# A gated linear recurrence and an MLP: the first batch's small gate operations on another engine, and a new order of all work

## The chip, the cores and the metric

The kernel runs on one core of one Trainium2 chip. A core has five engines that run their own instruction streams in order and meet through semaphores: TensorE (PE, matrix products), VectorE (DVE), ScalarE (ACT), GpSimd (POOL), and SyncE (SP), which here starts all DMA transfers. The metric is the device time in microseconds (us), the median over runs of the same program. A separate execution was profiled: its time is given beside the runs, and all durations come from it.

## What is computed

Two blocks follow each other. The first is a linear recurrence with complex decay, for 4 batches, 8 heads, 768 tokens and 48 channels. Cut to what matters:

```python
mag = np.sqrt(a_re * a_re + a_im * a_im)
scale = np.minimum(mag, 0.999) / (mag + 1e-06)
for t in range(S):                       # S_re, S_im: one 48 x 48 state per head
    new_re = ar * S_re - ai * S_im       # ar, ai: the scaled a_re, a_im of token t
    new_im = ar * S_im + ai * S_re
    S_re, S_im = new_re + kv, new_im     # kv: outer product of k and v of token t
    y[t] = q[t] @ S_re
```

The second takes the result as 3,072 tokens of 384 values and runs an MLP over it: `h = x @ w_in` (to 2,048 features), `g = max(h, 0) + alpha * min(h, 0)`, `g @ w_out` (back to 384).

## The kernel before

**Gates.** The decays are turned into running products. This is done in nine groups of tokens, `gates(g, b, c0, c1)`: chunks of 128 tokens 0, 1 to 2 and 3 to 5 of batch 0 are groups 0, 1 and 2; each later batch has two groups of three chunks. A group loads its slices of `a_re` and `a_im` (L248), normalizes them with ScalarE and VectorE (L251 to L308), and forms products over blocks: wide ones within blocks of 8 tokens, smaller ones over blocks of blocks, and a serial run over the ends of these (`product`, L336 and L338; the serial run is the loop over `nr`, which is 2, 4 and 6 steps long in groups 0, 1 and 2). Between these stages ScalarE makes negated copies (`three`, L364 and L366; L389). Then follow corrections of the offsets (L394, L397), a renormalization (L401 to L407), and the wide products L422 and L425. The decays go to `decs` in DRAM (L321), the rotations to `phs` (L417, L427). A `carry` links a group to the next of its batch.

**Who does the small operations.** `tiny` and `tiny_engine` (L230) choose an engine for a group's small operations: the products whose width is at most `SMALL` (80), the serial run, the offsets' corrections and the renormalization. In the kernel before it is VectorE for group 0 alone and GpSimd for the other eight.

**Units.** A unit is one chunk of 128 tokens, all heads; there are 24. `loads` brings q and k (`KQ`, three buffers), the rotations (`PP`, one buffer, L586) and the decays (`T`, two buffers, L593); `loads_v` brings v in the layouts that are needed. `unit(u)` then rotates KQ (L645), and goes through six levels of halves: TensorE multiplies (`ps_lv`, L659), VectorE multiplies KQ by decays (L698), ScalarE copies a half (`W`, L716), the products are masked (L680, L683). Then come transposes (`ps_kt`, L733), the new states (`ps_kv`, L746, with L754 and L757 on VectorE), and y, from the carried state (L773) and from the levels (L786). y goes to DRAM (`ysc`) and comes back transposed as `xT`.

**Weights.** `w_in` and `w_out` come as 64-bit numbers in 16 pieces (L487) and are turned into 32 bits by ScalarE (L503 to L507) and VectorE (L511 to L515).

**MLP.** The units' tokens are taken in 14 groups: two of one unit, ten of two, two of one. For each group and each of 16 blocks of 128 features, `features` runs three products (`ps_h`, L833), ScalarE a relu (L840) and VectorE the rest of the activation (L842); `outputs` adds up the 16 products with `w_out` (`ps_o`, L852), one block behind the features. `ps_h` has two buffers.

**The order.** Each of these tasks is a generator that yields between instructions. The string `ORDER` has one letter for each step (A to I: gate groups; J: loads; K: the copies of v into half rows; L: loads of v; M: weight loads; N and O: the two weight conversions; P to Z and a to m: units 0 to 23; n: loads of x; o: the MLP), and `plan.run(ORDER)` advances the named task. So the string fixes how every engine's queue is filled, and the DMA queue too. It was found beforehand by a search over a model with durations; the search isn't part of the kernel.

Of the kernel before, what the change touches and what calls it, by code (L numbers as in the profile page):

```python
# [27 lines left out]


ORDER = (  # L30
    "AAAAAAAAAAAAAAAMMAMJMMBJBAAAAAAAAAAAAAAAAAAAOOONNAAAAAAAAAAMAAAAAABNAAAAAAAAAAANAAAAABOAAAAAAAAJNABA"
    "ANAMBAAMAJAAAAAAAAAKNBBBBNNBBBBMBBBBBBBBBBBBCCBOOOBBBBBBBBBBBBBBBBBBBBBBBBBBBKJJJKONNOONOOPNCCCNNNBB"
    "OBOKPNNMNNNOOCONBBBBLLLBBBBBJPPPPPOCCKLKKLNNLPPCCCPCPPPKMKOCCPPCPOKKKKKBBBBBBBPBCBBBOBBJKPPOCMNPOONN"
    "NNBCMOJOLLLLCLPOMMMNPPPPPLLBBBBBBBCBCBBBBBBBNPCNCPJJLJDDJJPCCCJPKPCCCCCCCCCCCPPCCCPPPNCCCNCCCCCCCCPP"
    "NNPPJPPPOPNODJOPPPOJQDNPOPPCCCCCCPDQQQOQDDNNOODQQQOQDQQMJDCQCCCCCCQOODQJJDCQQQKDCDDDDCCCDCOnRCKKCKCD"
    "QooooJKKQQJJOooMJoQooooooCCCQCCLNDoRCCDooCRRRoOoooooooDQCRRDNoRooooooooooooDRQoKOQKQCRCoQLLLLQoDRooL"
    "oLoLLLLLLLQoQCCDDoRRDDJKQooMKCCCCCCNCDDQQQNoooQQCCoNQooooCoQQQQQQQQQQQQCDCooLNoOnoooJRRoORNoooOoooLo"
    "oooOooRooooJJJONDLRLDoEooooooOoooDoooooDooRooJooooooSRDoooooRRRRRooooRooRRooDLLLLLLLLLLoooEooJoDDSoo"
    "SoRSDSSoDDDRoSSoRoRoDooDSoDoRRRRRRJRoSEoSRERESERSRRRJJJoSSJToSESooooESSooSoRTEoSRDJDDDSSDKDSDDJDDDDD"
    "DDDDDDTESTTLDDRSSSToLLLooTLEoEDDDoETSooooLoLLJJLLLLLLoTSooEoSTRoooSoSEEESoSSSESSTKKDDDDDDKKDDDoDDDSS"  # L40
    "SSSESJJKoJoSJUJSSKooSoooDooooooTLLJnTETJLEEEKKEETJTDDEooDDDDooooooooLEUDEDooooToUUUDooEDTEoooLoooooo"
    "oUooTDTDLEooooTTTDTEDoooooTooooTUoooEoJooTLLoETETUoEDTTUUoUTooEooUoooEoEULLLLLLTTTTTTTEEJTooTTTTTTTJ"
    "FEEEFJEEEEUUoEoooooEEVooEoUUUUUUVVFoooooooUVUoUUFoTUUJTJEVVoFooFoEEEUUooooLUVUUVoVVFooVLLELLLLLLLLLL"
    "UUFEVoUEEEFUUUUUEUJVVJJJJVVUUoooUFUVJEEEVWoVoVVVVVEVVEooEooWJJEEEEEWoVoVoUoKWWVVVWVVVFWWFWFEEEoEEEoE"
    "EEFULLLLLLLLLLLLoLLVWVFVWWVVVVVVVWnVWFFJooooooEoWJJJJJWoLLLLLKoXLoooooWWoJWWWWEEEEWFooKooLLLLLLLoXEW"
    "WWooooVEEVoWEFVLWWEoooooEVJJJKWJVEoEEooWoWoWWVEWXoooooXooooooWWWWWWWFFFEXWWWWXoXJoXFLLLLLLFWWGGJJoWo"
    "FFFFoFFoFooFFooooXFoooXoXooFFoooXXXoXLXooLoFJooooKFFXooooGFFXooXGoGoXXXXooooGFoFYoGXoGooooFooooooYGG"
    "XXXGooooooGFFoooooooXGGoXLXGLJonYYYGooGooXXGFoFLoLFLFLoYXYXXYXoooXXXYoJJJJJYJJooooXFFFFFFFYYYXFXXGoo"
    "FFFFGGYGJoGooGGYGLLZLLLLLLLYLLoooLoLFLoooFYoooXFFYYFoooooGoJGGGGFFXGZYGYXYXFFYXXYYYYYooFFFFFoooGYYGG"
    "GGGZoooooYoFFFFFoFoooFoooYYZoYooZZGYYYYYYYJJJJJJoZZGGYYGoZFLGGLZLLLLZZFooooKLLLGJFFGJYaZooKFoFFKooGG"  # L50
    "GoFooYZoooGGZKFoooooFFoooooZZZoKZoYYZYYZZZZooooooLooLooaGGGGGZZooLFoZFFooLFoZGGZGGGGGGGGGnooooooZZoo"
    "ooooZaLaaZZFZaooaJaZoooZGaoaZZZZZZJJJGaGGGaaaaoJJJGGGGGGGJJGGabbaoooooLLLLLoooooooooooooooooooZGbZZo"
    "LLLLLLLLGbKaGHGaobobHZGGGZaaGGGoaboooooooooooooooaGaabaJaaooZoooGoGaboooaaaooooaabbbaabaaaGJbJaaJJbJ"
    "LbJHbaoLoocaaHboLooboJJooHoaaoHHoJKLbaoooHoobbbbbboooGoooooooooLocbbcoooHbbooooooHHHKHHLLHbLbLcooooo"
    "ooooLnooooLbobLLLcooHooobbbGIcccbJbcbIbbbbJbbbJJbbbbccJoooooooooooHHoHHccoIoooooccoooIodooHccooooooo"
    "HcLcdoooJooooHHHHHHHodcoJooooooccccddooccoccdddoocooccocLdLLooooLLLLLLLLJLLcdccdJJddcccHcccccccccccd"
    "eJdHooooHoooooooodJdHHHHooooooooddoeoddddeedoooooooooedHeoHddeIooooooddodoHIHHKooKoddeeooLLLLLLLLLLL"
    "LLLdddIneeeddedHddddddddeeeeooHHoJJoKJJJJfoJoIdKdJooooooooooIoHHoooodfIefoooeHHHHHHHHeooHooeofeeefJI"
    "oIoooooJooooooIIofeeHHHIHHIKoooeHeIfKJHHJoeoooHHHoooooooooooeHHHHHooHHHofeooLLLLLLLLLLLLLLJJofeeeeff"
    "ffeeeHHHHeeeeeeeeffgJJJfeKKKKoeLfoooHHJoHHoooooooHHooIgffHfLLLLLLLffLggLLffooKJLHooeoLoooooIgogfIgoI"  # L60
    "IIHoIfoHIIfILnHHHHoooooooooooooooKoofggoJfoofoooHoHooofooffHHHHHffoooooooooofooooooggIggIIIIIfffffff"
    "fIJgoILIoooooggoooogooJILILIILILLoogoIooLoggffgggooooffofoIIoIIhoooooogoooooooLoohIhhggggLLoooggJJLo"
    "oLLJJoogoooooooooJJJJIooogohhhggghggggJgIgIIIhhhhgggIIIggooIoohIIhLIIIIoioohgIIIoooooIIIIIIIIoohhhoo"
    "ooooJhhhhiiihhhLLLLhioLLooooooooIIILJihhLLJLIILIILIoioJoJLohhIhoJohhJiiohnoooiIihihhoooohjooooohhiIh"
    "IIhIIhhhJJhijiooLLIoioooIoIooooojIooooooooooooIojoooJooLoLLLLLLLLLiiijjjojhjooooooLooooooooIIIoooooi"
    "IIjiiiiJJijiioooooooooiiohLoooooohojohooJooihjiioooooiJJooiiiiiiiiiiiiiijJJLLioiJoLjJkojooLooooLoLLL"
    "oJjJonooLLooojLLJjkkjjkkjjoJLjoooooLoooooooojjjkkookooooojjoojoooojoojjjlkkjkkkjjjjjjjjjjjjjokkkJooo"
    "okoooooooooooolLLJkkooooooookkkkllkoooooooooolklkoolooLLllJoooooLLoooLLJoooooooLLkjkooooooooLoookkoo"
    "oookkooLooooooooLLkkokllJllkkJJkkkkkkkkJlkkkkooooooollooooooooomlooooooomJlllnJlolmmlLLLlooLmLLLLLLL"
    "LLoooooooLooloommoooloooolomlloooooloooloooooooolllmmlmmmllllllllmmoooooooooooooolmmllmmoomoommooooo"  # L70
    "oollloooooooooooooomomLooooooooooooooooooooooooooooooooooooommonoooooooooooommmoooooooooooooooooooom"
    "moLLooooooooooooooooooooLLLooLLooooooomoooLLLLoLmoomoooooooommmmmmmmmmmmmooooooooooooonooooooooooooo"
    "oooooooooooooooooooooooooooooooooooooooooooooooooooooooooooooooooooooooooooooooooooooooooooooooooooo"
    "oooooooooooooooo")

# [27 lines left out]
def kernel(  # L103
# [32 lines left out]
    nc = tc.nc  # L136
# [62 lines left out]
    DVE = ACT = POOL = PE = DMA = step  # L199
# [21 lines left out]
    def gates(g, b, c0, c1):  # L221
# [3 lines left out]
        first, last = c0 == 0, c1 == NCH  # L225
# [1 line left out]
        STT = nc.vector.scalar_tensor_tensor  # L227


        tiny, tiny_engine = (DVE, nc.vector) if b == 0 and first else (POOL, nc.gpsimd)  # L230

        def small(k, *after):
            return tiny(k, *after) if k <= SMALL else DVE(k, *after)
# [660 lines left out]
    with tc.manual_schedule():  # L894
        for i, g in enumerate(GATES):
            plan.add(gates(i, *g))
        plan.add(loads())
        plan.add(half_rows())
        plan.add(loads_v())
        plan.add(pieces())  # L900
        plan.add(weights("in"))
        plan.add(weights("out"))
        for u in range(NU):
            plan.add(unit(u))
        plan.add(loads_x())
        plan.add(all_mlp())
        plan.run(ORDER)
# [37 lines left out]
```

## Time and profile before

| | |
|---|---|
| median of 3 runs | 895.61 us (893.58 to 896.97) |
| the profiled execution | 889.42 us |
| its span, first to last instruction | 887.7 us |
| granted TensorE clock, mean | 0.962 |
| TensorE busy | 712.9 us (80%) |
| VectorE busy | 645.7 us (73%) |
| ScalarE busy | 428.0 us (48%) |
| GpSimd busy | 227.4 us (26%) |
| bytes moved by DMA | 130.98 MB, mean 148 GB/s |

The profile is a page of parts. The first gives each engine's busy time, its share of the span and its instructions. The second cuts the span into 40 equal slices; a digit is the busy share of a slice in tenths, and PEclk is the clock that TensorE was granted, in tenths of full speed. The third lists the DMA queues; queue 8 carries instructions. Behind the page lies the trace: what each engine waited for (with the time, the number of waits and the longest), sums over chosen stretches, and lists of instructions in order of time, with start, duration, engine, source line, operation, tiles and shapes. "issue" stands for time in which an engine waited for nothing that the profile shows. A matmul of 32-bit numbers appears as two records on PE and two weight loads on PEld.

### The profile page before, as it was taken

The numbers are of one execution on the slowest core, as the hardware profiler recorded it, in microseconds if no ns is written. First come the engines' busy times: TensorE is split into PE (matmuls) and PEld (weight loads), VectorE is DVE, ScalarE is ACT, GpSimd is POOL, SyncE is SP. The second block draws the span as 40 slices with busy tenths as digits, with TensorE's granted clock in tenths as the row PEclk, the third lists the DMA queues.
The fourth block names the chain that finished last, engine by engine and source line by source line (L and its number), as shares of the span: only waits on it lengthen the run. The fifth ranks groups of instructions, "written<-read, shape, count | busy, mean of one in ns | idle before, by whom it ended". The sixth has DMA issues, their size and how long they took to land.

```text
span 887.7 us, 28064 instructions
## 1 busy us (share of the span) xinstructions
PE 712.9 (80%) x12096; PEld 533.0 (60%) x12096; DVE 645.7 (73%) x941; ACT 428.0 (48%) x913; POOL 227.4 (26%) x347
## 2 busy tenths in 40 slices
PE   0001327877987799989899998999899999999998
PEld 0000326656665576767666776777677777777776
DVE  5989998978986799998586886789577664452212
ACT  7689485465455547633365644553332342223221
POOL 3066375037233201955100000630340000000000
PEclk9999958988998999999999999999999999999999
DMA  7777985986777789477786737567854744611110
GB/s 204 218 185 209 253 191 129 241 171 147 206 165 144 136 184 260 97 175 177 166 179 166 180 88 149 112 135 205 163 120 104 170 102 90 129 31 35 37 37 10
DMA packets 194562, 130.98 MB, mean 148 GB/s; under 512 B 74504, under 2 KB 186248, under 8 KB 194440
## 3 DMA queue, kind: packets, MB, share of 16 engines
q1 hardware_dynamic: 194440, 129.20, 62.2%
q8 instruction: 95, 1.56, 0.8%
q14 instruction: 27, 0.22, 0.1%
HBM read 100.82 MB, written 35.71 MB: 154 GB/s over the span
## 4 chain that ended last, share of the span: by engine, by line
PE 63%; DVE 16%; ACT 7%; issue 6%; POOL 3%; DMA 1%; DVEq 0%; ACTq 0%
PE ps_o L852 25%; PE ps_h L833 24%; PE ps_lv L659 5%; PE ps_y L786 4%; DVE KQ L698 4%; DVE gate L336 2%; PE ps_y L773 2%; PE ps_kv L746 2%; DVE gate L338 1%; PE ps_kt L733 1%; DVE gate L422 1%; DVE g_sb L842 1%; POOL gate L338 1%; DVE KQ L645 1%; DVE gate L296 1%
## 5 line engine op out<-in xcount | busy, mean ns | idle before, releaser
L852 PE MATMUL ps_o<-w_out_sb,g_sb 128*128 128x384 f32 x768 | 300.3, 505 | 12.4 <-DVE g_sb L842 12.2
L833 PE MATMUL ps_h<-xT,w_in_sb 128*128 128x256 f32 (+1 forms) x1344 | 307.2, 361 | 2.8 <-issue 2.8
L833 PEld LDWEIGHTS ps_h<-xT,w_in_sb 128*128 128x128 f32 x1344 | 237.8, 197 | 75.8 <-issue 8.2
L698 DVE TENSOR_TENSOR KQ<-KQ,T 96x1024 f32<-96x1024 f32 x144 | 177.9, 1243 | 65.9 <-PE ps_lv L659 61.0
L842 DVE SCALAR_TENSOR_TENSOR g_sb<-g_sb,al,ps_h 128x256 f32<-128x256 f32 (+1 forms) x224 | 97.0, 437 | 141.2 <-ACT g_sb L840 140.6
L840 ACT ACTIVATE g_sb<-ps_h 128x256 f32<-128x256 f32 (+1 forms) x224 | 78.8, 353 | 229.3 <-PE ps_h L833 228.6
L852 PEld LDWEIGHTS ps_o<-w_out_sb,g_sb 128*128 128x128 f32 x768 | 138.5, 193 | 63.9 <-DVE g_sb L842 15.6
L716 ACT COPY W<-KQ 96x512 f32<-96x512 f32 x120 | 74.4, 624 | 80.0 <-DVE KQ L698 77.1
L659 PE MATMUL ps_lv<-KQ,W 96*32 96x32 f32 x3840 | 58.1, 205 | 55.5 <-ACT W L716 43.7
L659 PEld LDWEIGHTS ps_lv<-KQ,W 96*32 96x32 f32 x3840 | 45.6, 117 | 78.5 <-ACT W L716 50.0
L336 POOL TENSOR_TENSOR gate<-gate 128x72 f32<-128x72 f32 (+1 forms) x56 | 35.9, 641 | 163.5 <-ACT gate L366 159.7
L786 PE MATMUL ps_y<-A,VL 64*48 64x64 f32 x2304 | 45.8, 229 | 20.0 <-issue 19.9
L659 PE MATMUL ps_lv<-KQ 96*32 96x32 f32 x768 | 12.1, 205 | 59.1 <-DVE KQ L645 57.7
L645 DVE TENSOR_TENSOR KQ<-KQ,PP 96x2048 f32<-96x2048 f32 x24 | 55.4, 2310 | 1.6 <-DMA PP<-phs 1.6
L799 ACT COPY yT<-ps_y 48x256 f32<-48x256 f32 x96 | 32.0, 366 | 48.1 <-PE ps_y L786 42.4
L786 PEld LDWEIGHTS ps_y<-A,VL 64*48 64x48 f32 x2304 | 39.7, 128 | 24.6 <-issue 22.6
L659 PEld LDWEIGHTS ps_lv<-KQ 96*32 96x32 f32 x768 | 9.4, 117 | 66.1 <-DVE KQ L645 57.8
L680 ACT ACTIVATE A<-ps_lv,rows 128x64 f32<-128x64 f32 x144 | 39.9, 331 | 16.7 <-PE ps_lv L659 16.3
L338 POOL TENSOR_TENSOR gate<-gate 128x36 f32<-128x36 f32 (+1 forms) x56 | 46.8, 835 | 4.3
L336 DVE TENSOR_TENSOR gate<-gate 128x576 f32<-128x576 f32 (+3 forms) x70 | 45.0, 642 | 2.0 <-ACT gate L366 0.5
L422 DVE TENSOR_TENSOR gate<-gate 128x1152 f32<-128x1152 f32 (+2 forms) x36 | 43.0, 1217 | 0.1
L336 POOL TENSOR_TENSOR gate<-run,runs 128x12 f32<-128x12 f32 x46 | 32.5, 706 | 36.7 <-ACT runs L366 33.9
(96 smaller groups left out, 774.1 us busy)
## 6 DMA issues: line engine op xcount, KB each, us to landing
T<-decs SPq DMA_DIRECT2D x48, 384.0 KB
PP<-phs SPq DMA_DIRECT2D x48, 193.5 KB
KQ<-in_q_dram SPq DMA_DIRECT2D x48, 192.0 KB
decs<-gate SPq DMA_DIRECT2D x7, 1152.0 KB
phs<-gate SPq DMA_DIRECT2D x14, 576.0 KB
KQ<-in_k_dram SPq DMA_DIRECT2D x40, 192.0 KB
vsc<-in_v_dram SPq DMA_DIRECT2D x48, 144.0 KB
VL<-vsc SPq DMA_DIRECT2D x24, 288.0 KB
```

What stands on the lines that cost most here:

```text
L336: on(4 * k).tensor_tensor(out=m, in0=w[:, 1::-1].unsqueeze(2).to_broadcast([P, 2, 2, k]), in1=pairs_of(u), op=ALU.mult)
L338: on(2 * k).tensor_tensor(out=dst, in0=m[:, 0], in1=m[:, 1], op=ALU.add)
L422: TT(out=m[:, a], in0=U5[:, 1 + a], in1=turned(off3, o)[:, a].unsqueeze(1).unsqueeze(3).to_broadcast([P, L // 2, nb, 2]), op=ALU.mult)
L645: nc.vector.tensor_tensor(out=KQ, in0=KQ, in1=bass.AP(tensor=PP.tensor, offset=PP.offset, ap=[PP.ap[0], (1, 2), (P + 1, H), (1, P)]), op=A ...
L659: nc.tensor.matmul(t[64 * i + j:64 * i + j + HC // 2, p], lhsT=weights(4 * i + p)[:, j:j + HC // 2], rhs=q_[:, m * g:m * (g + 1)], start=T ...
L698: nc.vector.tensor_tensor(out=x, in0=x, in1=m, op=ALU.mult)
L716: nc.scalar.copy(W.rearrange("p n t -> p (n t)").rearrange("p (m h) -> p m h", h=h), halves(KQ[:, 1].rearrange("p n t -> p (n t)"), h)[:, ...
L786: nc.tensor.matmul(o, lhsT=Vp[h][64 * i:64 * i + 64, s, e_ * D:(e_ + 1) * D], rhs=a, start=False, stop=(h == LEVELS[-1] and s == 1))
L833: nc.tensor.matmul(p, lhsT=w_in_sb[:, f // 2, kk, f % 2 * P:(f % 2 + 1) * P], rhs=x_of[m][:, kk], start=(kk == 0), stop=(kk == NK - 1))
L840: nc.scalar.activation(gt, p, AF.Relu, scale=-1.0)
L842: nc.vector.scalar_tensor_tensor(out=gt, in0=gt, scalar=al_1[:, f:f + 1], in1=p, op0=ALU.mult, op1=ALU.add)
L852: nc.tensor.matmul(sums[0], lhsT=gt[:, c * P:(c + 1) * P], rhs=w_out_sb[:, f], start=(f == 0), stop=(f == NF - 1))
```

## The change

In `gates`, the small operations of all groups of batch 0 go to VectorE: groups 1 and 2 besides group 0. The string `ORDER` is another one, from a new search; the durations in its model now include the arrival of instruction packets and TensorE's clock gate. Nothing else is changed: every task has the same steps, and only the two groups' small operations change their engine. The diff, with all but a few lines of the string left out:

```diff
 ORDER = (
-    "AAAAAAAAAAAAAAAMMAMJMMBJBAAAAAAAAAAAAAAAAAAAOOONNAAAAAAAAAAMAAAAAABNAAAAAAAAAAANAAAAABOAAAAAAAAJNABA"
-    "ANAMBAAMAJAAAAAAAAAKNBBBBNNBBBBMBBBBBBBBBBBBCCBOOOBBBBBBBBBBBBBBBBBBBBBBBBBBBKJJJKONNOONOOPNCCCNNNBB"
...
+    "AAAAAAAAAAAAAAAAAAAAABBAAAAMBBAAAAMMMMMAAAAAAAAAAAAAAANBBNAAAAJJAAAAAAAAJAOONMNAOAAAAOAAAANAAAAAAAA"
+    "AOMAAAAAABBNAABNAAAAAKJBAANNBNBMBBBBBBBBCNBBBBBBBBBBNBBOOOOBBBBBBBBBBBBNNCBBOJMOBCCCOONBBBBBBBBBBBBB"
...
@@ gates
-        tiny, tiny_engine = (DVE, nc.vector) if b == 0 and first else (POOL, nc.gpsimd)
+        tiny, tiny_engine = (DVE, nc.vector) if b == 0 else (POOL, nc.gpsimd)
```

## The prediction

> **What bounds the kernel now.** The page first: where TensorE (PE) idles, and which engine is full then.
>
> ```profile
> PE 712.9 (80%) x12096; PEld 533.0 (60%) x12096; DVE 645.7 (73%) x941; ACT 428.0 (48%) x913; POOL 227.4 (26%) x347
> PE   0001327877987799989899998999899999999998
> DVE  5989998978986799998586886789577664452212
> POOL 3066375037233201955100000630340000000000
> PEclk9999958988998999999999999999999999999999
> q8 instruction: 95, 1.56, 0.8%
> ```
>
> A slice is 22 us. PE is nearly empty for six of them while VectorE (DVE) is full; from slice 14 on PE is full. So I cut at milestones: the MLP's 224 features (16 for each of 14 token groups), each seen as one L842 on DVE. Feature 0 is at 134 us, feature 48 at 306, the end at 887.7. The sums over two stretches, then PE's waits in the first and in the second:
>
> ```profile
> 134.00:306.00 172.00, 138.92 (x2842) 104.89 (x2843) 144.58 (x204) 90.78 (x200) 63.80 (x91) 0.90 0.74 167
> 306.00:888.00 582.00, 555.73 (x8660) 412.75 (x8658) 385.98 (x539) 238.15 (x572) 98.16 (x163) 0.99 0.56 127
> ```
> ```profile
> PE ps_o L852 <- DVE g_sb L842: 12.2, 9, 5.4
> PE ps_y L786 <- issue: 10.1, 4, 4.2
> PE ps_lv L659 <- issue: 5.0, 2, 3.9
> ```
> ```profile
> PE ps_y L786 <- issue: 9.8, 10, 3.8
> PE ps_lv L659 <- issue: 5.4, 4, 2.9
> PE ps_h L833 <- issue: 2.8, 1, 2.8
> PE ps_y L773 <- issue: 2.4, 1, 2.4
> ```
>
> Columns of the first fence: PE, PEld, DVE, ACT, POOL busy, clock, DMA share, GB/s. After 306 us PE is the bound, and all but 2.0 us of its waits are "issue" (20.4 us): it waited for nothing but its own instructions. Between 134 and 306, issue is 15.1 us and the clock 0.90. Three limits in turn, then: DVE up to feature 0, DVE and PE together up to 48, PE with its instruction supply after that.
>
> **What the Trainium skill says.** "Runtime: NRT & Kernel Launch", Instruction fetch mechanics: instructions come in 16 KiB blocks of 256, and crossing a block is mostly hidden. The trace has the blocks (95 packets, 1.56 MB) and contradicts the rest: 35.5 us of issue after 134. "TensorE: Matmul & The Clock Gate", Part 1: an idle array runs at half clock, decided in windows of 3.4 us. It agrees: half-clock stretches of 3.4 and 6.8 us follow the stalls, and one of 27 us (109 to 136) covers the thin attention work. "SBUF — State Buffer", Who interferes with whom: a DVE instruction with two SBUF inputs locks out a GpSimd (POOL) one that reads SBUF. The same 128x12 product on both engines agrees:
>
> ```profile
> 66.53 0.23 POOL L336 TENSOR_TENSOR gate<-run,runs 128x12 f32<-128x12 f32 x1
> 68.11 1.34 POOL L336 TENSOR_TENSOR gate<-run,runs 128x12 f32<-128x12 f32 x1
> ```
> ```profile
> 24.54 0.17 DVE L336 TENSOR_TENSOR gate<-run,runs 128x12 f32<-128x12 f32 x1
> 24.74 0.17 DVE L338 TENSOR_TENSOR run<-gate 128x6 f32<-128x6 f32 x1
> ```
>
> **The moved operations.** 71 instructions (gate groups 1 and 2) leave POOL for DVE. DVE's rows for their kind in group 0 run from 0.17 to 0.25 us, and 0.55 at 384 columns for the few wide ones: 71 x 0.2 = 14 us more on DVE, 12 at the least, 18 at the most. Hidden after feature 48, where DVE is busy 386 of 582; paid in full before feature 0. POOL's chain for group 1 ran from 48.7 to 83.9 us and for group 2 from 103.6 to 148.0; on DVE such a chain took 8 us (20.4 to 28.3). Every instruction of ScalarE, PE and SP is still there, 755 DMAs among them, in another order. New on DVE are the waits for ScalarE inside these chains: L336 for L366 (twice per group), L394 for L389, L403 for L401. Whatever stands behind them on DVE waits too: weights (L511 to L515), the next gates, from group 2 on the units' L698 and with them PE. In the built order one to three other instructions stand in each such place (group 1: L511 and L513; L257 and L511; L385 and L513; L515), 0.7 to 2 us against 0.5 to 1 us of ScalarE. So I take nothing; without the cover it would be 8 places at up to 1 us.
>
> **The order up to feature 0.** I add, over what stands ahead of an instruction in DVE's order, each row's mean. Ahead of the first L842 before: gates 67.3, weights 27.0, units 26.7, other 1.6: 122.6, and it began at 134.0, 11.4 later (9.5 of that is the start-up, already there at the first L645: 42.5 against 52.0). After: gates 103.3, weights 27.0, units 46.6, other 1.6: 178.4. Three units' attention and more gates now come first. 178.4 + 11.4 = 189.8: the MLP begins 56 us later. Beside this hide ScalarE (130.5 us of sum) and DMA (32.9 MB ahead of the first x load, at the 210 GB/s of the first slices 157 us).
>
> **Feature 0 to 48.** PE's prices are start-to-start times, as here (6 features and 4 outputs in 2.59 us):
>
> ```profile
> 806.64 1.46 PE L833 MATMUL ps_h<-xT,w_in_sb 128*128 128x256 f32 x6
> 807.94 1.45 PE L852 MATMUL ps_o<-w_out_sb,g_sb 128*128 128x384 f32 x4
> 809.23 1.46 PE L833 MATMUL ps_h<-xT,w_in_sb 128*128 128x256 f32 x6
> ```
>
> 0.67 for 6 features of 128 columns; per unit 2.34 for the levels, 0.66 and 1.02 for transposes and states, 2.5 for y. The whole order sums to 668.1 in both. Between features 0 and 48 PE has 114.8 before and 103.0 after; DVE 156.5 and 108.8. Before, 0.93 of DVE's sum is busy time (144.6 of 156.5), so after DVE needs 101: PE now sets the pace, and the two are almost equal. Instruction supply: when PE stalls, packets follow each other at 4.0 to 4.3 us (278.85 and 283.10, 391.97 and 396.02). So I cut PE's order into blocks of 256 (a matmul is 4) and count for each block what its work falls short of 4.05 us. Before this gives 35.5 us past feature 0 (8.8 up to 48, 26.7 after), against 35.5 us measured (15.1 and 20.4): right in sum, loose by stretch. After: 7.6 up to 48. The half clock costs about 5 at the start (before, 10 us of MLP ran so) and 1.7 for one window; short idle gaps 6 (before some 9 for 115 us); waits for DVE 2, by the stretch 306 to 363, where DVE needs 56 (0.93 x 60.2) and took 57; PE is a feature ahead, -1.3. Sum: 189.8 + 103.0 + 7.6 + 6.7 + 6 + 2 - 1.3 = 313.8, 7.8 later than now.
>
> **Feature 48 to the end.** Before: 544.1 of work, 20.4 issue, 2.0 other waits, 5.1 for three half-clock windows, rest about 10: 581.5. After: work 548.7; short blocks 11.0 instead of 26.7 (10 of them instead of 19), times 20.4/26.7, is 8.4; waits 2; two windows 3.4; rest 6.5, because some of the 10 went with the stalls: 569.0.
>
> **Sum.** 313.8 + 569.0 = 882.8, 4.9 less than the span of 887.7. The profiled execution took 889.42, so 884.5; the median of the runs, 895.61, lies 6.2 above that execution, and I carry the difference over: **890.7**. This is the likeliest case, 887 to 897, at 0.48. It straddles the bound of 0.5% (about what a measurement of this kernel can tell from none, 891.1): 0.24 faster, 0.24 same.
>
> **Rivals.** (1) Slower: in the stretch to feature 48 the two equal engines wait for each other. Both run in order; an L842 behind a 2.3 us L645 or a 1.24 us L698 holds L852, and L698 waits for ps_lv behind the MLP. Before, PE lost 23 us there to such waits, with PE less loaded. At 18 instead of 2: 907. It decides for slower from 12 us. For it: equal sums. Against: from 306 to 363 near-equal sums cost 1 us. Chance 0.18. (2) The stalls stay, because they hang on the DMA load at their time and not on the order: 12 more late (20.4 for 8.4), 7 early (15.1 for 7.6), some 4 of it in time in which PE waits for DVE anyway: 906. For it: the count misses each stretch by 6 us. Chance 0.11: slower 0.09, same 0.02. (3) Faster: the equal stretch runs at PE's work and stalls alone, and the late rest shrinks with the stalls: 6 + 2 + 6 less, 877. For it: the long unbroken MLP keeps the clock up. Chance 0.20. (4) The early sum is too small: the second unit's L645 stands 12.9 us behind the first, and PP has one buffer; reloading took 7.6 us from issue to use (164.9 to 172.5), 10.6 are left, so 0 to 5. Or DMA gives 167 GB/s: the first x at 197. 5 to 10 us, 898: chance 0.03, slower. That the move doesn't take place is excluded: the built order has 1014 DVE instructions for 943.
>
> **Chances and range.** Faster 0.24 + 0.20 = 0.44; same 0.24 + 0.02 = 0.26; slower 0.30. The range 875 to 907 leaves out 0.08 below (the farther half of rival 3's cases) and 0.12 above. The likeliest case alone is 887 to 897.
>
> **What would show it.** POOL empty from 10 to over 100 us; first L833 near 188 us, L842 number 48 near 314; PE issue below 20 us after it starts; fewer half-clock windows; PE without gaps from 314 on. Wrong if the first L842 is before 180 or after 200, if L852 waits over 12 us for L842, or if issue stays above 30.

## The result, and the profile after

The changed kernel takes **866.1 us** (median of 4 runs, 864.91 to 868.58), the kernel before beside it 894.6 us (4 runs, 892.61 to 896.97). The ratio is 0.968, with a 95% interval of 0.965 to 0.972. It is faster by 28.5 us; 890.7 was predicted, with a range of 875 to 907. A second set of runs gave 866.7 (864.46 and 869.0) against 894.9. Here and below the medians are of all runs, while a ratio leaves out the runs that lie over 1.5% above the fastest of the same kernel.

The profiled execution of the changed kernel took 868.58 us with a span of 866.9. The milestones of the prediction, read in the same way (start of the L842 of that feature, in us), with a second profile of each kernel:

| | feature 0 | 16 | 48 | 64 | 96 | end |
|---|---|---|---|---|---|---|
| before | 134.0 | 172.2 | 306.2 | 363.0 | 490.1 | 887.7 |
| before, second profile | 134.0 | 174.5 | 307.9 | 365.2 | 496.1 | 894.4 |
| predicted after | 189.8 | | 313.8 | | | 882.8 |
| after | 177.3 | 221.5 | 294.7 | 348.6 | 471.7 | 866.9 |
| after, second profile | 177.5 | 221.1 | 294.0 | 348.1 | 473.1 | 867.3 |

The MLP starts 43 us later, is 12 us ahead at feature 48, and gains another 9 by the end. The page of the kernel after, the busy times and the slices (22 us each):

```profile
PE 703.0 (81%) x12096; PEld 527.9 (61%) x12096; DVE 653.4 (75%) x1012; ACT 428.6 (49%) x913; POOL 156.4 (18%) x276
PE   0000233488999999999999998999999999999998
DVE  5999999987977998899989875897667755434212
POOL 3000002293024103400175033010520000000000
PEclk9999999678999999999999999999999999999999
q8 instruction: 95, 1.56, 0.8%
```

PE (TensorE) is now at 4 tenths or less for eight slices instead of six, but then runs at 9 in nearly every slice. Before, a stretch of 7 and 8 followed. GpSimd (POOL) lost 71 us of busy time, its 71 instructions of batch 0; VectorE (DVE) gained 71 instructions and only 7.7 us (653.4 for 645.7). The instruction packets are the same 95. The sums over the three stretches (PE, PEld, DVE, ACT, POOL busy, then clock, DMA share, GB/s):

```profile
0.00:177.00 177.00, 35.31 (x1189) 29.51 (x1194) 162.67 (x318) 121.56 (x184) 25.01 (x43) 0.95 0.80 206
177.00:294.00 117.00, 109.25 (x2008) 85.73 (x1995) 99.15 (x148) 62.19 (x152) 43.38 (x70) 0.95 0.68 165
294.00:867.00 573.00, 558.42 (x8921) 412.62 (x8919) 391.55 (x548) 244.86 (x578) 87.97 (x163) 1.00 0.56 131
```

DVE is busy 162.67 of the first 177 us; before it was 115.18 of 134. PE is busy 109.25 of the middle 117; before, 138.92 of 172. PE's waits in the middle stretch, and then in the last (total, times, longest, in us):

```profile
PE ps_kt L733 <- ACT KT L737: 3.6, 1, 3.6
PE ps_o L852 <- DVE g_sb L842: 0.4, 1, 0.4
PE ps_y L786 <- issue: 0.2, 1, 0.2
PE ps_h L833 <- issue: 0.2, 1, 0.2
```
```profile
PE ps_lv L659 <- issue: 3.8, 4, 1.8
PE ps_y L786 <- issue: 3.4, 3, 1.8
PE ps_h L833 <- DMA xT<-ysc: 2.5, 2, 2.0
PE ps_h L833 <- DVE g_sb L842: 0.3, 1, 0.3
```

The waits of L852 for L842 in the middle stretch, 12.2 us before, are 0.4, and "issue" there is nearly gone (15.1 before). In the last stretch issue is 7.2 for 20.4. The moved products of group 1, on VectorE after (start, duration):

```profile
55.38 0.18 DVE L336 TENSOR_TENSOR gate<-run,runs 128x12 f32<-128x12 f32 x1
55.59 0.17 DVE L338 TENSOR_TENSOR run<-gate 128x6 f32<-128x6 f32 x1
```

0.18 us each, as the rows of group 0 said; on GpSimd the same form took from 0.23 to 1.34.

Where PE lost time, in three stretches: up to feature 0, from 0 to 48, from 48 to the end. "Half" is the time at half clock. The experiments below stand with the kernels, since the table is used for them too. One profile is one execution: that of early part new fell on its slowest of 20 runs (902.01, median 894.6), that of move alone on its slowest of 4, that of order alone on its fastest.

| us | issue | other waits | half | length |
|---|---|---|---|---|
| before | 0, 15.1, 20.4 | 110.8, 22.8, 2.0 | 23.9, 34.1, 10.2 | 134.0, 172.2, 581.5 |
| before, second | 0, 16.4, 24.8 | 110.7, 24.2, 1.9 | 1.1, 29.6, 13.9 | 134.0, 173.9, 586.4 |
| after | 4.5, 0.4, 7.2 | 137.2, 7.2, 2.9 | 18.5, 12.3, 4.9 | 177.3, 117.4, 572.2 |
| after, second | 4.5, 2.0, 7.9 | 137.2, 4.6, 2.7 | 0, 6.8, 3.8 | 177.5, 116.6, 573.2 |
| order alone | 4.0, 0, 6.6 | 142.1, 6.7, 2.3 | 55.8, 12.4, 3.4 | 181.5, 117.7, 569.5 |
| move alone | 0, 14.3, 25.8 | 122.1, 26.1, 1.2 | 22.4, 39.0, 27.4 | 145.7, 175.9, 593.6 |
| early part new | 1.9, 4.9, 25.7 | 140.1, 8.0, 1.8 | 18.6, 25.8, 24.5 | 177.6, 133.4, 589.3 |
| late part new | 0, 15.2, 8.0 | 110.7, 23.3, 5.2 | 1.1, 36.5, 6.9 | 134.1, 178.6, 567.9 |

Over the whole span PE's waits and issue fall from 171.1 to 159.4 us, and in the second profiles from 178.0 to 158.9. That is 11.7 of the 20.8 us by which the span shrinks, and 19.1 of 27.1. PE has the same instructions in both kernels, so the other 8 to 9 us lie in the time that these took: after feature 0 PE has 27 and 33 us less at half clock.

### The profile page after: what moved, and what is told of

Same layout as the page of the kernel before. It is cut to its first block, busy times and chain, and to the rows that moved or that the text cites. A ratio compares the mean times of both kernels' runs of the same rounds, so it can differ in the third digit from the quotient of the medians.

```text
span 866.9 us, 28079 instructions
## 1 busy us (share of the span) xinstructions
PE 703.0 (81%) x12096; PEld 527.9 (61%) x12096; DVE 653.4 (75%) x1012; ACT 428.6 (49%) x913; POOL 156.4 (18%) x276
## 4 chain that ended last, share of the span: by engine, by line
PE 68%; DVE 13%; POOL 5%; DMA 5%; ACT 3%; issue 3%; SPq 2%; DVEq 0%; ACTq 0%; POOLq 0%
PE ps_h L833 27%; PE ps_o L852 27%; PE ps_lv L659 5%; PE ps_y L786 4%; POOL gate L336 2%; PE ps_y L773 2%; PE ps_kv L746 2%; DVE gate L336 2%; DMA xT<-ysc 2%; DVE KQ L698 2%; PE ps_kt L733 1%; DVE gate L338 1%; DMA T<-decs 1%; POOL gate L338 1%; POOL run L338 1%
## 5 line engine op out<-in xcount | busy, mean ns | idle before, releaser
L833 PE MATMUL ps_h<-xT,w_in_sb 128*128 128x256 f32 (+1 forms) x1344 | 304.1, 357 | 4.9 <-DMA xT<-ysc 4.3
L852 PE MATMUL ps_o<-w_out_sb,g_sb 128*128 128x384 f32 x768 | 292.9, 495 | 0.5 <-DVE g_sb L842 0.4
L833 PEld LDWEIGHTS ps_h<-xT,w_in_sb 128*128 128x128 f32 x1344 | 233.1, 193 | 74.6 <-DMA xT<-ysc 2.6
L698 DVE TENSOR_TENSOR KQ<-KQ,T 96x1024 f32<-96x1024 f32 x144 | 176.5, 1230 | 45.4 <-PE ps_lv L659 40.2
L842 DVE SCALAR_TENSOR_TENSOR g_sb<-g_sb,al,ps_h 128x256 f32<-128x256 f32 (+1 forms) x224 | 97.5, 437 | 125.6 <-ACT g_sb L840 125.0
L852 PEld LDWEIGHTS ps_o<-w_out_sb,g_sb 128*128 128x128 f32 x768 | 136.5, 190 | 50.1 <-DVE g_sb L842 1.6
L659 PE MATMUL ps_lv<-KQ,W 96*32 96x32 f32 x3840 | 57.5, 205 | 40.8 <-ACT W L716 31.9
L659 PE MATMUL ps_lv<-KQ 96*32 96x32 f32 x768 | 12.2, 206 | 95.1 <-DMA g_sb<-in_w_in_dram 71.6
L659 PEld LDWEIGHTS ps_lv<-KQ,W 96*32 96x32 f32 x3840 | 45.4, 117 | 66.2 <-ACT W L716 43.9
L659 PEld LDWEIGHTS ps_lv<-KQ 96*32 96x32 f32 x768 | 9.7, 119 | 100.2 <-DVE KQ L645 89.8
L336 POOL TENSOR_TENSOR gate<-gate 128x72 f32<-128x72 f32 x42 | 26.8, 637 | 137.0 <-ACT gate L366 134.2
L336 DVE TENSOR_TENSOR gate<-gate 128x576 f32<-128x576 f32 (+5 forms) x84 | 48.8, 581 | 2.5 <-ACT gate L308 0.6
L786 PE MATMUL ps_y<-A,VL 64*48 64x64 f32 x2304 | 44.1, 231 | 3.7 <-issue 3.7
L786 PEld LDWEIGHTS ps_y<-A,VL 64*48 64x48 f32 x2304 | 39.2, 130 | 8.0 <-issue 6.1
L422 DVE TENSOR_TENSOR gate<-gate 128x1152 f32<-128x1152 f32 (+2 forms) x36 | 43.0, 1215 | 0.1
L683 DVE TENSOR_TENSOR A<-ps_lv,mask 128x256 f32<-128x256 f32 x96 | 39.5, 413 | 0.0
L303 POOL MEMSET gate<- 128x18 f32 (+2 forms) x9 | 1.0, 112 | 192.8 <-DVE gate L296 148.3
```

The lines of the kernel that those rows point to most:

```text
L336: on(4 * k).tensor_tensor(out=m, in0=w[:, 1::-1].unsqueeze(2).to_broadcast([P, 2, 2, k]), in1=pairs_of(u), op=ALU.mult)
L422: TT(out=m[:, a], in0=U5[:, 1 + a], in1=turned(off3, o)[:, a].unsqueeze(1).unsqueeze(3).to_broadcast([P, L // 2, nb, 2]), op=ALU.mult)
L659: nc.tensor.matmul(t[64 * i + j:64 * i + j + HC // 2, p], lhsT=weights(4 * i + p)[:, j:j + HC // 2], rhs=q_[:, m * g:m * (g + 1)], start=T ...
L698: nc.vector.tensor_tensor(out=x, in0=x, in1=m, op=ALU.mult)
L786: nc.tensor.matmul(o, lhsT=Vp[h][64 * i:64 * i + 64, s, e_ * D:(e_ + 1) * D], rhs=a, start=False, stop=(h == LEVELS[-1] and s == 1))
L833: nc.tensor.matmul(p, lhsT=w_in_sb[:, f // 2, kk, f % 2 * P:(f % 2 + 1) * P], rhs=x_of[m][:, kk], start=(kk == 0), stop=(kk == NK - 1))
```

## The experiments

The theory was the prediction's, with its sizes open: the order carries the gain, in an early part (VectorE's work ahead of the MLP instead of beside it) and a late part (fewer short blocks of instructions, so fewer issue stalls and half-clock windows). The rivals: the moved operations carry it; or the late gain has nothing to do with instruction supply. Medians and ratios are against the kernel before in runs beside them (894.9 to 897.2 us).

### One part of the change at a time

The move in the old order:

```diff
 # on the kernel before
-        tiny, tiny_engine = (DVE, nc.vector) if b == 0 and first else (POOL, nc.gpsimd)
+        tiny, tiny_engine = (DVE, nc.vector) if b == 0 else (POOL, nc.gpsimd)
```

> The order string of the kernel before, with the small operations of groups 1 and 2 on VectorE. Theory (the gain is the order's, in VectorE's first 180 us and in PE's instruction supply after 300 us): VectorE's sum up to feature 48 grows from 279 to 293 us and nothing that it waited for goes away, so 5 to 12 us slower than before; PE's issue waits stay near 35 us. Rival (the move is the gain: GpSimd's chain held the first units back): 10 us or more faster.

Measured: 913.8 us (910.73 to 917.0), ratio 1.020 (1.015 to 1.025). It costs 19 us.

The new order with the old choice of engine:

```diff
 # on the kernel after
-        tiny, tiny_engine = (DVE, nc.vector) if b == 0 else (POOL, nc.gpsimd)
+        tiny, tiny_engine = (DVE, nc.vector) if b == 0 and first else (POOL, nc.gpsimd)
```

> The new order string, with the small operations of groups 1 and 2 left on GpSimd. Theory: the new order puts group 1's later gate work only a few us behind its small operations in VectorE's queue, so GpSimd's chain (35 us for group 1 before, 44 for group 2) blocks VectorE; feature 0 comes 20 to 50 us later than after the change, and the time is 10 to 40 us above it, that is around or above the kernel before. Rival (the move does nothing for the time, the order everything): within 3 us of the kernel after the change, 866.

Measured: 875.2 us (870.48 to 876.11), ratio 0.976 (0.971 to 0.981). The order alone gains 20 us. So the same edit of one line costs 19 us in the old order and gains 9 in the new one (875.2 to 866.1; the runs of the two don't overlap). Both sizes were missed: 5 to 12 were expected for the one, 10 to 40 for the other. Up to feature 0 the traces show why they differ. In the old order VectorE's sum ahead of the first L842 grows from 122.5 to 133.3 and the first L842 comes 11.7 later: paid in full. The other 7 us lie behind it, past feature 48 above all (593.6 for 581.5 to 586.4), with 27 us at half clock instead of 10 to 14; why the clock fell there isn't settled. In the new order without the move, VectorE's waits up to 178 us:

```profile
DVE gate L422 <- POOL gate L407: 7.4, 1, 7.4
DVE KQ L698 <- PE ps_lv L659: 6.6, 2, 3.8
```

The chain on GpSimd stands ahead of VectorE's wide products (L422), which wait 7.4 us for it. The same view of the kernel after has no such wait:

```profile
DVE gate L257 <- ACT gate L255: 5.5, 1, 5.5
DVE KQ L698 <- PE ps_lv L659: 0.4, 1, 0.4
```

Without the move VectorE has 71 instructions less, and its first L842 is still 4.2 us later (181.5 for 177.3). So GpSimd's chain accounts for some 4 of the 9 us. The rest isn't seen in the profiles, whose ends lie only 1.9 us apart, because that of order alone fell on its fastest run; what it is stays open.

### The early and the late part apart

The order was cut just ahead of the L842 of feature 48: first the steps of one order up to there, then those steps of the other that have not been made, in its sequence. The first changed line of each string:

```diff
 # early part new, on the kernel after: the old order's sequence from feature 48
-    "EoELLLWEEEoELoEELJVKoJVJoFoooEEVoEVEoooooEoVoVooEoooVEVVWVVooooFoJJFFoooooooVXFVVWFooVWVVFWWoLJLVVJV"
+    "EoELLLWEEEoELoEELJVKoJVJoFoooEEVoEVEoooFFFVVFFFFVVFVWWVVVVVVVWVWFFWWoLLLLLoXLoooooWWoJWWWWWFooKooLLL"
...
 # late part new, on the kernel before: the new order's sequence from feature 48
-    "EEFULLLLLLLLLLLLoLLVWVFVWWVVVVVVVWnVWFFJooooooEoWJJJJJWoLLLLLKoXLoooooWWoJWWWWEEEEWFooKooLLLLLLLoXEW"
+    "EEFULLLLLLLLLLLLoLLVWVFVWWVVVVVVVWnVWFFJooooooEoWJJJJJWEEEEEEEEKEEEEooEooooEoooEoooooJJoooooooXoooLJ"
...
```

> The new kernel up to feature 48 (small operations on VectorE), from there on the remaining steps in the order of the kernel before. Theory: the gain up to feature 48 (306.2 to 294.7 us in the two profiles, 11.5) is kept and the late one lost, since the blocks of 256 instructions past feature 48 fall short by 24.4 us again: 10 to 15 us faster than before, issue waits after feature 48 about 20 us. Rival (the late order is no gain in itself): 25 us or more faster than before. Rival (the early gain is an accident of the cut and is given back later): no faster.

Measured: 894.6 us (888.75 to 902.01, 20 runs), ratio 1.000 (0.998 to 1.003).

> The kernel before up to feature 48 (small operations on GpSimd), from there on the remaining steps in the new order. Theory: the late gain (581.5 to 572.2 us past feature 48, 9.3) appears alone: the blocks past feature 48 fall short by 12.4 us instead of 26.7; issue waits there near 8 us, at most one or two half-clock windows, 8 to 15 us faster than before. Rival (stalls hang on the DMA load and not on the order): issue waits near 20 us and no gain.

Measured: 881.5 us (879.39 to 885.4), ratio 0.984 (0.979 to 0.989).

The late part stands alone: from feature 64 to the end 518.8 us, as in the kernel after (518.3 and 519.2), for 524.7 and 529.2 before. PE's waits for issue past feature 48 with the late part new, and then in the second profile of the kernel before:

```profile
PE ps_lv L659 <- issue: 4.6, 5, 2.2
PE ps_y L786 <- issue: 3.4, 3, 1.7
```
```profile
PE ps_y L786 <- issue: 13.3, 9, 4.3
PE ps_lv L659 <- issue: 7.1, 3, 3.7
```

8.0 us in all, for 24.8 there (the two lines are 20.4 of it). The early part lost everything that was expected of it (10 to 15 us), as its second rival had it. At the cut the steps that the new order had put off and the old one has before feature 48 stand in a clump: VectorE's sum ahead of that L842 is 298.1 instead of 287.2. The sums of the profile over the 17 us in which the kernel after had already passed feature 48:

```profile
294.00:311.00 17.00, 9.92 (x276) 8.43 (x274) 14.38 (x17) 9.48 (x12) 0.00 (x0) 0.80 0.55 140
```

PE is busy 9.92 of 17 us, at a clock of 0.80. Feature 47 still stands at 293.7 us (290.3 in the kernel after, 298.8 before); feature 48 follows 17.2 us later, where the kernel after takes 4.4. So the loss belongs to the seam, the clump at the cut, and the total says nothing of the early gain. So the cut was moved to feature 96, both ways, with a repetition of both kernels beside it for milestones:

```diff
 # new up to 96, on the kernel after
-    "occcGocboHcoocooHobcHKGJGGGGGGGGoooHLHHboLbooooooooLGGGGKGoooooobboLGoGobooooHoGKbGooooooGGoboooooob"
+    "occcGocboHcoocooHobcHKGJGGGGGGGGoooHLHHbGGGGGGGGGGGbbbbbbLLLbbbGIbbbIbbbbbbbJJbbbbcJooooooooccoIoooo"
...
 # old up to 96, on the kernel before
-    "ooooLnooooLbobLLLcooHooobbbGIcccbJbcbIbbbbJbbbJJbbbbccJoooooooooooHHoHHccoIoooooccoooIodooHccooooooo"
+    "ooooLnooooLbobLLLcooHooobbbGIcccbJbcbIbbbbJbbbJJbbbbccJooooHHHHHHHHHHKKHHHHHHHHHKHHHoooooooooKoooooo"
...
```

> The new kernel up to feature 96, then the remaining steps in the order of the kernel before. In the two profiles feature 96 stood at 490.1 and 471.7 us, the rest took 397.6 and 395.2. Theory (the early part gains by itself, some 14 to 18 us; the cut at 48 lost it because the two orders stand at different points there): 870 to 882 us, feature 96 near 472, blocks past 96 fall short by 17.6 us instead of 5.0 and give some 10 us more of issue waits. Rival (the early lead is only work put off, paid back later): 888 us or more.

> The kernel before up to feature 96, then the remaining steps in the new order. Theory (supply of instructions in the rest): blocks past 96 fall short by 9.5 us instead of 19.8, so 5 to 10 us faster than before. Rival (all of the late gain lies ahead of feature 96 or needs the new early part): within 3 us of before.

> The kernel before once more, for a second profile: its first one took 889.4 us where its runs have a median near 895. If that execution was one with fewer stalls, this profile, nearer the median, has more than 35.5 us of issue waits past feature 0 or more than 44 us at half clock there. If the difference lies outside the span, issue waits and clock are as before.

> The changed kernel once more, for a second profile: its first one took 868.6 us and its runs have a median of 866.1. Expected within 3 us of that, with issue waits of 6 to 14 us past feature 0, because the order leaves few places where they can arise.

Measured: new up to 96 888.7 us (883.32 to 894.38, 20 runs), ratio 0.998 (0.995 to 1.001); old up to 96 896.0 us (890.82 to 902.56, 13 runs), 1.004 (1.000 to 1.008); before 892.7 (887.33 to 899.45, 18 runs), 1.000; after 866.7, 0.976 (0.964 to 0.989). The runs of before beside them have a median of 894.9; one of the 48 took 1827.19 us, for a reason that isn't known, and is left aside. By the means of all the other runs, new up to 96 is 5.6 us faster than before (888.9 for 894.6, give or take 2); the ratio hides this, because it leaves out the upper third of before. Both theories missed (870 to 882 us, and 5 to 10 us faster): in both cases the rival's number came out.

| us | feature 64 | 64 to 96 | 96 to end |
|---|---|---|---|
| before, two profiles | 363.0, 365.2 | 127.1, 130.9 | 397.6, 398.3 |
| after, two profiles | 348.6, 348.1 | 123.1, 125.0 | 395.2, 394.2 |
| new up to 96 | 345.6 | 137.6 | 398.4 |
| old up to 96 | 360.2 | 144.5 | 389.5 |

The early lead is there in three profiles, 14 to 20 us at feature 64, and the whole new order does not give it back. That of new up to 96 fell on its fastest run. Up to feature 95 it is level with the kernel after (466.6 us in both); then feature 96 takes 16.6 us where the kernel after takes 5.1. In old up to 96 it is 22.4, for 9.3 and 10.6 before. So both cuts again lose some 12 us at the seam, to steps that one order had put off and the other had made. A hybrid's total is no measure of either part. What can be read from cuts is a stretch away from the seam: feature 64 to the end behind a cut at 48, and feature 64 ahead of a cut at 96. They give 14 to 20 us early and 6 to 10 late. These are places in time and not causes: by the prediction's prices PE has 4.6 us more work behind feature 48 in the new order (548.7 for 544.1), so that much of the early lead is work put off, and the late stretch gains in spite of it.

### Instruction supply, by filling and by moving

If the late gain is supply, then instructions that add almost no work cost a block's 4.05 us per 256 where blocks are short, and nothing where they are long. So 480 small matmuls (96x32) were added between the L786 of units 9 to 23, and in another kernel between the L852 of groups 4 to 11. Their products go into columns of the PSUM tile that nothing reads (`YF` and `sums[1]` are the whole tiles):

```diff
 # dense, on the kernel after: behind each L786 with h <= 8, from unit 9 on
+                            [nc.tensor.matmul(YF[0:32, 0, 256:288], lhsT=KQ[:, 1, 0, 0:32], rhs=KQ[:, 0, 0, 0:32], start=False, stop=False) for _ in range(1) if u >= 9 and h <= 8]
 # sparse, on the kernel after: behind each L852, two for one
+        [nc.tensor.matmul(sums[1][0:32, 384:416], lhsT=w_in_sb[0:96, 0, 0, 0:32], rhs=w_in_sb[0:96, 0, 0, 32:64], start=False, stop=False) for _ in range(2) if 4 <= m < 12 and f < NF - 1]
```

> The new kernel with 480 extra 32-column matmuls on PE (24 ns each by the trace, 4 instructions each, results unused), put between the y products (L786) of units 9 to 23, where the instruction stream is dense already. Nothing else is touched; the output is the reference's. Theory (PE's supply of blocks of 256 instructions bounds the dense places): past feature 48 the blocks fall short of 4.05 us by 28.3 us instead of 11.0, so besides the direct 12 us some 12 to 17 us of issue waits and one to four half-clock windows more: 24 to 35 us above 866. Rival (issue waits hang on DMA load, not on instructions per time): only the direct 12 us, and issue waits as before near 12 us.

> The same 480 matmuls put between the output products (L852) of token groups 4 to 11, where the instruction stream is thin. Output as the reference's. Theory: the blocks fall short by 18.1 us instead of 11.0, so the direct 12 us and 3 to 7 us of issue waits: 13 to 20 us above 866, and 8 to 18 us below the dense case. Rival: the same time as the dense case.

Measured: dense 1150.5 us, ratio 1.283 (1.277 to 1.290); sparse 974.9 us, 1.087 (1.082 to 1.093). Theory and rival both had taken a filler at 0.024 us of PE's time, and both missed. By the spans it cost 0.59 us in the dense place (1149.9 - 866.9 over 480) and 0.22 in the sparse one (972.6 - 866.9 over 480). The groups of the dense kernel (busy, mean ns; idle before):

```profile
L786 PE MATMUL ps_y<-A,VL 64*48 64x64 f32 x2304 | 228.9, 283 | 1.4 <-issue 1.4
L787 PE MATMUL ps_y<-KQ 96*32 96x32 f32 x960 | 141.3, 237 | 0.0
```

L786, which took 44.1 us in the kernel after, takes 228.9, and issue past feature 48 is 7.8, no more than without the fillers. So the time did not go to instruction packets. The clock was at half for 291 us there, and the matmuls no longer run one over another: a record of L786 is 283 ns long for 231 before the fillers came in, but the time that the records cover is five times as long. What both kernels have in common is the change from one tile shape to another and back around the fillers. In the sparse one it shows in the fillers' weight loads:

```profile
L853 PEld LDWEIGHTS ps_o<-w_in_sb 96*32 96x32 f32 x960 | 48.5, 111 | 133.4 <-issue 133.4
```

241 waits of 0.55 us in the mean, one for each of the 240 pairs of fillers, where a block of 256 instructions would give one for every 64 matmuls. That it is the shape, and not the shared bank of PSUM or another trait of the fillers, can be read from the kernel after, which has such changes of its own. PE there:

```profile
208.52 0.83 PE L833 MATMUL ps_h<-xT,w_in_sb 128*128 128x128 f32 x6
209.19 0.81 PE L852 MATMUL ps_o<-w_out_sb,g_sb 128*128 128x384 f32 x2
209.83 0.83 PE L833 MATMUL ps_h<-xT,w_in_sb 128*128 128x128 f32 x6
210.50 0.81 PE L852 MATMUL ps_o<-w_out_sb,g_sb 128*128 128x384 f32 x2
211.24 0.46 PE L659 MATMUL ps_lv<-KQ,W 96*32 96x32 f32 x32
211.63 0.94 PE L833 MATMUL ps_h<-xT,w_in_sb 128*128 128x128 f32 x6
212.40 0.81 PE L852 MATMUL ps_o<-w_out_sb,g_sb 128*128 128x384 f32 x2
```

From the start of L852 to the next start 0.64 us pass ahead of L833 and 0.74 ahead of a level (L659); the six L833 take 0.67, and 0.77 behind the level. In medians past feature 48, start to start: the last L852 ahead of a level 416 ns for 322, the first L852 behind one 427. Ahead of and behind a pair of fillers it is 416 and 427 too, and the pair itself takes 242: 94 + 242 + 105 is 441 ns, and two fillers cost 440. So what is dear is the change of tile shape, some 0.2 us there and back outside the small matmuls themselves. A level spreads this over 16 matmuls, the fillers over two. In the dense kernel the half clock comes on top; that part wasn't separated.

As a test of supply both runs are void. The test that was left was a placement: the old order of everything else, with the MLP's steps set where the new order has them (by the number of other steps ahead of each; 55 of the 1,552 stand up to 26 steps later).

```diff
 # MLP later, on the kernel before
-    "QooooJKKQQJJOooMJoQooooooCCCQCCLNDoRCCDooCRRRoOoooooooDQCRRDNoRooooooooooooDRQoKOQKQCRCoQLLLLQoDRooL"
+    "QJKKQQJJOMJQCCCQCCLNDRCCDCRRRODQCRRDNRDRQKOQKQCRCQLLLLQDRLLLLLLLLLQQCCDDRRDDJKQMKCCCCCCNCDDQQQNQQCCN"
...
```

> The old order of all steps but the MLP's, small operations of groups 1 and 2 on GpSimd, and the MLP's steps put after as many other steps as in the new order (so the MLP starts later and then runs denser). VectorE's sum ahead of feature 0 is 166.5 us instead of 122.6, blocks past feature 48 fall short by 8.2 us instead of 26.7. Theory (the early gain comes from starting the MLP when VectorE can keep up with it, so that PE stays at full clock and runs short blocks beside a wait): feature 64 near 350 us instead of 363, and with the late gain 15 to 25 us faster than before. Rival (the early gain needs the move and the new order of the gates): feature 64 near 363 us, and only the late 8 to 14 us.

> The same with the small operations of groups 1 and 2 on VectorE. Theory: in the old order of the gates the move costs VectorE time and takes away no wait: 10 to 19 us slower than the kernel with the late MLP alone, as the move alone cost 19. Rival (the move pays once the MLP starts late): faster than it by 5 us or more.

Measured: 1041.4 us, ratio 1.160 (1.155 to 1.165), and with the move 1052.8, 1.172 (1.166 to 1.179). 15 to 25 us faster was expected. PE's largest wait in it, over the whole span:

```profile
PE ps_lv L659 <- ACT W L716: 103.5, 42, 8.0
```

In the kernel before this wait is 4.4 us past feature 0; here it is 45.0 of the 103.5. There the units' levels stand between the MLP's products, and ScalarE's copy W is mostly done when PE comes back to them. Moved by count, that fine mesh is gone, and PE waits 42 times for it. Nothing follows for the theory, except that a late MLP is not enough, and that the move costs 11 us in this order as well.

What an issue wait ends on can be read from the traces, though, without another run. Count PE's instructions (matmuls, weight loads and those of its sequencer) in the order of their starts, and set the end of each issue wait beside the packets of queue 8. After feature 0 the kernel before has 22 such waits, 35.5 us. Each stands at instruction 192 or 193 of a block of 256, and ends 1.19 to 1.77 us after a packet has come in. The kernel after has nine, 7.6 us, at the same two places, 1.28 to 1.92 us after a packet. In the two repeated profiles, in the two halves of the change, and in the four kernels that are put together from both orders, all 118 of these waits stand at the two places as well, and end 1.19 to 1.84 us after a packet. Of the waits of over 0.4 us for another engine or a load, 8 of 138 in these ten profiles end 1.1 to 2.0 us after one, and none in the first profiles of the kernels before and after. So issue after feature 0 is the wait for the next block of instructions. In the kernels with the MLP later this holds for 8.9 of the 15.6 us past feature 48, and with the move for 6.8 of 13.5.

There is also a count. Past feature 48, the prediction's rule (blocks of 256 instructions, what their work falls short of 4.05 us) against the measured issue:

| us | rule | issue |
|---|---|---|
| before, two profiles | 26.7 | 20.4, 24.8 |
| move alone | 26.2 | 25.8 |
| early part new | 24.4 | 25.7 |
| late part new | 12.4 | 8.0 |
| after, two profiles | 11.0 | 7.2, 7.9 |
| order alone | 10.8 | 6.6 |

Six orders fall into the two groups that the rule names. The cuts at 96 do so as well: past feature 96 the issue is 1.5 us with the late part new (9.9 and 11.0 before), and 9.9 with it old (3.7 and 4.0 after). MLP later fits with its 8.9 (the rule has 8.2). The fillers do not (28.3 by the rule and 7.8 measured; 18.1 and 10.8): there the time of the matmuls was far more than the prices that the rule adds up. Nor are 4.05 us a floor: the closest packets of the kernel before are 3.3 us apart.

Between the two kernels the stretch shrank by 9 to 13 us and its issue by 13 to 17, so shorter waits for instructions are enough to account for the late gain, 4.6 us of added work included. That they are its cause is argued from these sums: no run changed the supply alone. What the half-clock time adds (5 and 10 us less of it) isn't separated from them.

## Why the prediction was wrong

The mechanism was the one described, and the sum was made of the right terms: VectorE's order sets feature 0, PE's work the middle, PE with its supply the end. GpSimd is empty from slice 1 to slice 5, issue after feature 0 is 7.6 (0.4 and 7.2) and not above 30, and L852 hardly waits. By its own test, a first L842 before 180, it was wrong. Its sign of a first L833 near 188 us failed too (161.2). Four terms of the sum were mis-sized, three of them the same way. Together they are the 24.6 us between 890.7 and 866.1.

**"The order up to feature 0": 189.8, measured 177.3 (-12.5).** The sum ahead of the first L842 was right: 178.4 predicted, 177.9 by the records of this profile. Wrong was to add the 11.4 us of before as a constant. It is a difference of two things: VectorE's idle time, and the time by which the records of neighbouring instructions lie over each other.

| us up to feature 0 | sum of records | overlap | idle | feature 0 |
|---|---|---|---|---|
| before | 122.5 | 7.3 (94 pairs) | 18.8 | 134.0 |
| after | 177.9 | 14.9 (185 pairs) | 14.3 | 177.3 |
| order alone | 164.4 | 11.8 (148 pairs) | 28.9 | 181.5 |
| move alone | 133.3 | 9.1 (112 pairs) | 21.5 | 145.7 |

So the offset is 18.8 - 7.3 = 11.5 before and 14.3 - 14.9 = -0.6 after. The overlap doubled. The Trainium skill, "Perfetto Trace Analysis", Summary: the profiler window per engine type, has it that a record of VectorE runs from the start in the ALUs until the write is acknowledged. That the next instruction can start inside this window is what the trace shows, where the next one doesn't need the result: of the 140 neighbours in the kernel after where the later one waits for the other and reads the tile that it wrote, 10 overlap; of the other 178, 176 do. VectorE in the kernel after, in order of time:

```profile
99.68 0.74 DVE L336 TENSOR_TENSOR gate<-gate 128x576 f32<-128x576 f32 x1
100.35 0.41 DVE L683 TENSOR_TENSOR A<-ps_lv,mask 128x256 f32<-128x256 f32 x1
100.68 1.21 DVE L698 TENSOR_TENSOR KQ<-KQ,T 96x1024 f32<-96x1024 f32 x1
101.81 0.44 DVE L338 TENSOR_TENSOR gate<-gate 128x288 f32<-128x288 f32 x1
102.18 0.54 DVE L511 TENSOR_SCALAR top<-top 128x768 f32<-128x768 f32 x1
102.65 0.74 DVE L336 TENSOR_TENSOR gate<-gate 128x576 f32<-128x576 f32 x1
103.43 0.46 DVE L338 TENSOR_TENSOR gate<-gate 128x288 f32<-128x288 f32 x1
```

The L683 and L698 of a unit start 0.07 and 0.08 us before the end of the record ahead of them, and so do the gates' L338 behind a unit's L698 and the weights' L511. The L338 at 103.43 follows directly on its own L336 (102.65 + 0.74 = 103.39) and starts 0.04 behind it. Over the whole stretch the median overlap is 0.08 us and the median small gap 0.035, in all four kernels. The new order mixes gates, weights and three units more finely, and each change between them is worth about 0.11 us (0.08 and 0.035): 91 more pairs overlap. Idle time went down by 4.5: in the order before there are 11 gaps over 0.2 us, 14.1 in all. Two at the start hold 7.8 of it; in the others VectorE waited up to 1.4 us at a time for units, weights and gates. After, four are left (8.4), and the same two hold 7.6. The prediction saw the new waits of the moved chains covered, and they were.

**"Feature 0 to 48": 124.0, measured 117.4 and 116.6 (-7).** PE's 103.0 held: with issue 0.4, other waits 7.2 and half of the 12.3 us at half clock it makes 116.8. Rival 1 fell: equal engines did not wait for each other (L852 for L842: 0.4 us, where 18 was its price). The term that failed is the 7.6 for short blocks. Issue was 0.4 and 2.0. Two others nearly cancel in the first profile: waits are 7.2 for 2, and what remains for gaps and PE's lead is 0.6 for 6 - 1.3. The rule has five short blocks there. Three of them, 4.4 us together, it puts at PE's features 1 and 2 (PE's L833 run ahead of VectorE's L842). They hold the last levels of a unit, its transposes, states and y. PE in order of time there (idle time before the instruction in brackets), and the last line a later y for comparison:

```profile
170.14 0.65 PE L659 MATMUL ps_lv<-KQ,W 96*32 96x32 f32 x32 [2.55 <-ACT W L716]
173.01 0.66 PE L659 MATMUL ps_lv<-KQ,W 96*32 96x32 f32 x32 [0.90 <-ACT W L716]
176.50 1.61 PE L746 MATMUL ps_kv<-V,KT 64*32 64x48 f32 x96 [0.66 <-DMA KQ<-in_k_dram]
179.91 2.81 PE L786 MATMUL ps_y<-A,VL 64*48 64x64 f32 x96
205.86 1.59 PE L786 MATMUL ps_y<-A,VL 64*48 64x64 f32 x96
```

The work of these blocks is 2.7, 2.6 and 2.4 us by the rule's prices. The time that passed was more: PE waited 2.55, 0.90 and 0.66 us for ScalarE and a load, and this y took 2.81 us at half clock where the later one took 1.59. By the trace's own count of instructions, the block that ends at 177.6 us took 7.0 us and the next one 4.3, and no issue wait stands there. In the second profile they took 7.0 and 4.3 as well, at full clock, with one wait of 0.3. A shortfall that is counted from work alone is too large wherever the engine is held up by something else. The other two blocks (3.2 us, features 30 and 43) cost 0.4 in one profile and nothing in the other, which has 1.7 of its 2.0 us ahead of feature 8, where the rule has no short block.

**"Feature 48 to the end": 569.0, measured 572.2 and 573.2 (+3 to +4).** This term is right within 1%. The 8.4 for short blocks measured 7.2 and 7.9. What is too small is the rest of 6.5, which was to shrink with the stalls: 548.7 of work, issue, other waits and half of the time at half clock leave 11 and 12. Before, it was about 10, so it hangs on something else. The trace has 206 changes of tile shape there, for 187 before; whether these make up the rest wasn't tested. Rival 2, stalls that hang on the load and not on the order, is refuted by 7.2 instead of 20.

**"Sum": the 6.2 carried over (-8.7).** The profile of before fell on one of its faster executions: 889.4, where runs go from 883.7 to 903.9 and the second profile took 896.1, with 41.1 us of issue after feature 0 instead of 35.5: 5.7 of the 6.7 us between the two spans. The profile of after fell on the slowest of its four (868.58, median 866.1). A distance between a profile and a median is the scatter of one kernel, and the stalls that scatter are what the change removed; carried over it was 8.7 too much.

In the span that makes -12.5 - 6.6 + 3.2, or -15.9 us by the first profile; the carry adds -8.7. The range's lower end, 875, came from rival 3 and was as blind to the first term as the sum. Rival 3 was on the right side, with its stretch at PE's work alone (877), but it too started from 189.8. The move's price of 12 to 18 us "paid in full before feature 0" was 10.8 us of VectorE's sum in the old order. That it would be worth 9 us in the new one, some 4 of them because GpSimd's chain would there stand in VectorE's way, wasn't seen, since the two edits were summed and never priced apart.

What stays open: how the early lead divides. From feature 0 to 48 issue fell by 14 to 15 us, other waits by 16 to 20 and the time at half clock by 22 to 23, while the waits ahead of feature 0 grew by 31. Up to feature 48 PE's waits and issue are thus 149.3 us for 148.7, and 148.3 for 151.3 in the second profiles: its idle time moved ahead of the MLP and hardly shrank. The lead of 11.5 to 13.9 us there is then 4.6 of work put off and, for most of the rest, less time at half clock. This is a sum from the traces; no run changed one of these alone.

## What to carry to other kernels

Split an offset into idle time and overlapping records before carrying it to another order, and count how many neighbours are independent: here that was worth 12 us of 178. A short block of instructions costs time only where nothing else holds its engine up, and the distance of one profile from a median belongs to that kernel alone. Price an edit in the order that it will stand in: the same line of code was worth +19 us in one order and -9 in the other, and pieces of two orders put together lost up to 13 us at the seam.

## What the runs showed of the hardware that was not expected

- Small matmuls strewn between those of another tile shape are dear. A 96x32 product between products of 64x48 tiles cost 0.59 us, half clock included (480 of them: 283 us), and between products of 128x128 tiles 0.22 us (106 us), where 0.024 was expected. The change from 128x128 tiles to 96x32 and back costs 0.09 and 0.10 us in the kernel after too, outside the small products.
- A wait for instructions can be told by its place: after feature 0 all 31 of the kernels before and after stand at the same position of a block of 256 of PE's instructions (192 or 193), and end 1.2 to 1.9 us after an instruction packet.
- Neighbouring VectorE instructions that don't depend on each other overlap by 0.08 us in the median, dependent ones stand 0.035 apart. 71 instructions more with 15.4 us of records raised VectorE's busy time by 7.7: the other records became 4.1 us shorter, and the overlaps 3.6 longer.
- The stalls for instructions are 35 to 41 us of the kernel before past feature 0, with up to 4.3 us at a time, and scatter between runs; the kernel with few of them has runs from 864.5 to 869.0, that with many from 883.7 to 903.9.
